# Linear attention and an MLP mixer on one core: attention by quarters of the array, three of nine token-mixing tiles summed onto x in PSUM, and the last block product added onto u

## The chip, the cores and the metric

The kernel runs on one core of a Trainium2 chip. The metric is device time in microseconds. A core has TensorE (PE; its weight loads are listed apart as PEld), VectorE (DVE), ScalarE (ACT), GpSimd (POOL), and SyncE (SP), which here issues nearly all DMAs. [...]

## The reference

```python
kv = einsum('bhsd,bhse->bhde', k, v)          # batch 8, heads 8, seq 576, head_dim 64
out = einsum('bhsd,bhde->bhse', q, kv)
rms = sqrt(mean(out * out, axis=-1) + 1e-6)
x = (out / rms * g_norm) as (8, 576, 512)
h = maximum(x^T @ w_tok1, 0) @ w_tok2          # 576 -> 256 -> 576 along the sequence
u = x + h^T
y = u + maximum(u @ w_ch1, 0) @ w_ch2          # 512 -> 1536 -> 512
```

q, k, v and the results are float32; the four weights come as float64 and are turned into float32 on the chip.

## The kernel before, in words

The work has two parts. The first (up to about 205 us) makes u; the second (up to the end) applies the two channel products by a fast block scheme of two levels, with seven products in the place of eight at each level. The change touches the first part and the last block product of the second.

**First part.** Batches go in pairs: pair 0 to 3, each with two batches ("sides"). The sequence of 576 is four tiles of 128 and a rest of 64; the rests of the two sides share one tile, so a pair has nine tiles of x, 128x512 each. Chunk c of 0 to 3 holds two tiles (sides 0,0,1,1), chunk 4 the shared rest.

For a pair the steps have short names, and the plans `start`, `middle`, `steady(...)` (twice) and `last` are lists of these names, written out by hand. The order of the names is the order in which every engine gets its instructions.

- `kv00` to `kv11` (side, half of the heads): the 64x64 products of k and v, two heads at once, into the two lower or upper column halves of the array (`128*64` in the profile). `l00` to `l11` load the next pair's k and v into the same buffers, `lq0`, `lq1` the next q. `e00` to `e11` copy the result to `kvp`, on DVE for pair 0, on ACT later.
- `a`: attention, q times kv, into an "o" bank. `kvp` holds two heads as a block diagonal of 128x128 with zeros, so that one matmul serves two heads. The zeros come from two memsets of the kv banks at the start.
- `g`: times g_norm, from the bank into x (DVE). `q`: square, from the same bank (ACT). `t`: sum over a head (DVE). `m`, `r`, `i`: mean, root (ACT), inverse (DVE), for a group of chunks. `s` or `p`: x times the inverse, by eight small ACT instructions or one of POOL.
- `h00` to `h11` and `hr` (side, half of the 256): the first token product, into four "h" banks, with the rest's part in `hr` and then a ReLU on ACT. `h010` is one fourth of `h01`.
- `u0` to `u8`: the second token product of one tile into an "h" bank (two matmuls of 128x512; for `u8` four that use half the columns), then x = bank + x on DVE, then a DMA to `u_dram` after each second tile.
- A digit n: n steps of decoding channel weights (ACT once, DVE six times a block). `w..`: the same for token weights. `j14`, `j10`, `j6`, `j2`: so many matmuls of an identity. `c0` to `c4`: transposes of u for the second part. A name with "-" belongs to the pair before.

In `middle` and `steady` the attention of pair n+1 is woven into the token mixing of pair n; `last` has the token mixing of pair 3 alone.

[...] two for "o", two for kv, four for "h". An "h" bank goes round: the fifth tile that asks for one waits until the first has been read.

**Second part.** `outer(place, size, mul, to, ...)` puts one outer block product on a time line of places: seven inner products into banks a, b and c, and between them copies (ACT) and additions (DVE) that leave four results in `to`. For the last group (the rests, g = 8) and the last block product (o = 3) `to` is a buffer r; `last(m, n)` then adds each quarter of r onto xg, and `store_rest` sends tiles of xg out, one half by a DMA of SP and one by a DMA that ACT issues.

Of the kernel before, what the change touches and what calls it, by code (L numbers as in the profile page):

```python
# [19 lines left out]
def kernel(  # L20
# [32 lines left out]
    nc = tc.nc  # L53
# [21 lines left out]
    def pool(name, bufs, side="left", stack=ctx, **kw):  # L75
# [16 lines left out]
          for n, b in (("o", 2), ("kv", 1), ("h", 4))}  # L92
# [10 lines left out]
    kvp = [inp.tile([P, HP, P], F32, name=f"kvp{i}") for i in range(2)]  # L103
# [227 lines left out]
    def attention(pair, groups):  # L331


        acc, bank, stat = {}, {}, {}

        def kv(side, half):
            n = 4 * pair + 2 * side + half
            kk, vv = k_in[n % 4], v_in[n % 4]

            for i in range(2):  # L340
                for j in range(JJ):
                    for h in range(2):
                        r = ds(h * D, D)
                        matmul(kv_ps[half][r, i, r], lhsT=kk[:, j, ds(i * P + h * D, D)],
                               rhs=vv[:, j, ds(i * P + h * D, D)],
                               start=(j == 0), stop=(j == JJ - 1), skip_group_check=True)

        def evict(side, half):
            o = kvp[side][:, 2 * half:2 * half + 2]
            if pair == 0:  # L350
                keep(nc.vector.tensor_copy(o, kv_ps[half]))
            else:
                copy(o, kv_ps[half])

        def attend(c, t):
            side = c // 2
            o = bank[c, t] = ps["o"].tile([P, DM], F32, name="ps_o", tag="o")
            for hp in range(HP):
                matmul(o[:, ts(hp, P)], lhsT=qT[2 * pair + side][:, hp, ts(2 * (c % 2) + t, P)],
                       rhs=kvp[side][:, hp], start=True, stop=True)  # L360

        def attend_rem():
            o = bank[4, 0] = ps["o"].tile([P, DM], F32, name="ps_r", tag="o")
            for hp in range(HP):
                for side in range(2):
                    matmul(o[ds(side * HF, HF), ts(hp, P)],
                           lhsT=qT[2 * pair + side][:, hp, LO:],
                           rhs=kvp[side][:, hp], start=True, stop=True)

        heads = lambda t: t.rearrange("p (h d) -> p h d", d=D)  # L370
        number = lambda c: H if c == 4 else 2 * H
        sq = {}

        def gain(c, t):
            if t == 0:
# [3 lines left out]
            keep(nc.vector.tensor_mul(heads(X[pair, c][:, t]), heads(bank[c, t]),  # L379
                                      g_sb.to_broadcast([P, H, D])))  # L380

        def square(c, t):
            sq[c, t] = work.tile([P, H, D], F32, name="sq", tag="sq", bufs=3)
            keep(nc.scalar.activation(sq[c, t], heads(bank[c, t]), AF.Square))
# [4 lines left out]
        def stats_of(c):  # L389
            g = group(c)  # L390
            at = sum(number(i) for i in g if i < c)
            return [t[:, ds(at, number(c))] for t in stat[g]]

        def total(c, t):
            g = group(c)
            if g not in stat:
                stat[g] = [stats.tile([P, sum(map(number, g)), 1], F32, name=name)
                           for name in ("ms", "root", "inv")]
            keep(nc.vector.tensor_reduce(stats_of(c)[0][:, ts(t, H)], sq[c, t], axis=AX.X,  # L399
                                         op=ALU.add))  # L400
# [20 lines left out]
        def scale(c, t):  # L421
            x, inv = heads(X[pair, c][:, t]), stats_of(c)[2][:, ts(t, H)]
            for i in range(H):
                keep(nc.scalar.activation(x[:, i], x[:, i], AF.Copy, scale=inv[:, i]))  # L424

        def scale_pool(c, t):
            x, inv = heads(X[pair, c][:, t]), stats_of(c)[2][:, ts(t, H)]
            keep(nc.gpsimd.tensor_mul(x, x, inv.to_broadcast([P, H, D])))
# [7 lines left out]
        for c in range(5):  # L436
            for t in range(1 if c == 4 else 2):
                steps |= {f"{n}{c}{t}": do(f, c, t) for n, f in
                          zip("agqtsp", (attend if c < 4 else lambda c, t: attend_rem(), gain,
                                         square, total, scale, scale_pool))}  # L440
# [5 lines left out]
    def token_mixing(pair):  # L446
# [19 lines left out]

        def tok2(i):
            acc_u = ps["h"].tile([P, DM], F32, name="ps_u", tag="h")
            if i < 8:
                for t in range(NTOK):  # L470
                    matmul(acc_u, lhsT=w_tok2[:, t, ts(i % J, P)], rhs=h1[i // J][:, t],
                                     start=(t == 0), stop=(t == NTOK - 1))
            else:
                for t in range(NTOK):
                    for side in range(2):
                        matmul(acc_u[ds(side * HF, HF)], lhsT=w_tok2[:, t, LO:],
                                         rhs=h1[side][:, t],
                                         start=(t == 0), stop=(t == NTOK - 1))
            x = x_of(pair, i)
            tensor_add(x, acc_u, x)  # L480
# [8 lines left out]
        steps |= {f"h01{j}": do(tok1, 0, 1, (j,)) for j in range(J)}  # L489
# [204 lines left out]
    def outer(place, size, mul, to, base=None, act=copy):  # L694
# [31 lines left out]
        def write(i, j, name, n):  # L726
            tensor_add(to(i, j), fit(banks[name]), t[n])
# [13 lines left out]
        at(2, "c", False, True, lambda: act(to(0, 0), fit(banks["c"])))  # L741
        put(place + PLACE[7] + 2, do(write, 1, 1, "b", "u3"))
        at(4, "a", False, True, lambda: read(to(1, 0), 1, 0))
# [448 lines left out]
```

## Time and profile before

| | |
|---|---|
| median of 3 runs | 813.27 us (813.24 to 813.54) |
| profiled execution | 813.68 us, of which span 811.9 us |
| TensorE clock granted | 0.999 |
| PE busy | 796.3 us, 6388 records |
| DVE busy | 690.8 us, 1318 instructions |
| ACT busy | 288.2 us, 805 instructions |
| DMA | 175.43 MB, 216 GB/s over the span |
| one chunk's tile, gain `g` (DVE, 128x512 from PSUM) | 681 ns, 32 times |
| square `q` (ACT, 128x512 from PSUM) | 597 ns, 32 times |
| x = bank + x (DVE, 128x512) | 678 ns, 36 times |
| copy of kvp (ACT, 128x256) | 356 ns, 12 times |
| scaling `s` (ACT, 128x64) | 335 ns, 184 times |

The span runs from the first to the last instruction; the device time has 1.8 us more around it. A line of the profile names the source line, the engine, the operation, what it writes and reads, and its shape. A form such as `128*64 128x64` of a matmul says: 128 rows and 64 columns of the array, and 64 columns of moving data on 128 partitions. `x16` is the number of records; a float32 matmul leaves two. What stands in brackets is the engine's idle time before, and what ended it. Most lines name one of the helpers (`matmul` is L127, `tensor_add` L118, `copy` L124, `dma` L115), so one goes by the names of tiles. TensorE's durations overlap from one record to the next; the distance of the starts is what a matmul costs.

### The profile page before, as it was taken

The numbers are of one execution on the slowest core, as the hardware profiler recorded it, in microseconds if no ns is written. First come the engines' busy times: TensorE is split into PE (matmuls) and PEld (weight loads), VectorE is DVE, ScalarE is ACT, GpSimd is POOL, SyncE is SP. The second block draws the span as 40 slices with busy tenths as digits, with TensorE's granted clock in tenths as the row PEclk, the third lists the DMA queues.
The fourth block names the chain that finished last, engine by engine and source line by source line (L and its number), as shares of the span: only waits on it lengthen the run. The fifth ranks groups of instructions, "written<-read, shape, count | busy, mean of one in ns | idle before, by whom it ended". The sixth has DMA issues, their size and how long they took to land.

```text
span 811.9 us, 16377 instructions
## 1 busy us (share of the span) xinstructions
PE 796.3 (98%) x6388; PEld 704.9 (87%) x6388; DVE 690.8 (85%) x1318; ACT 288.2 (35%) x805; POOL 79.9 (10%) x75
## 2 busy tenths in 40 slices
PE   6999999999999999999999999999999999999997
PEld 6655565543888899999999999999999999999996
DVE  4688989999986978988997997897898899799687
ACT  1355566471120134243234233333424323423331
POOL 1210101010000011003003003001100200300300
PEclk9999999999999999999999999999999999999999
DMA  9999998335458477368558638737836855764642
GB/s 294 324 342 329 341 357 290 131 130 169 166 203 294 169 213 244 131 210 256 174 182 247 211 134 270 238 118 249 268 123 213 249 178 190 239 199 136 202 147 82
DMA packets 97341, 175.43 MB, mean 216 GB/s; under 512 B 7024, under 2 KB 54128, under 8 KB 97264
## 3 DMA queue, kind: packets, MB, share of 16 engines
q1 hardware_dynamic: 95584, 172.65, 65.4%
q10 hardware_dynamic: 1680, 1.74, 0.7%
q8 instruction: 50, 0.82, 0.4%
q14 instruction: 27, 0.22, 0.1%
HBM read 137.79 MB, written 36.57 MB: 215 GB/s over the span
## 4 chain that ended last, share of the span: by engine, by line
PE 88%; DVE 7%; DMA 3%; issue 1%; ACT 0%; SPq 0%; ACTq 0%; DVEq 0%
PE ps_a L127 37%; PE ps_b L127 18%; PE ps_c L127 9%; PE ps_u L127 5%; PE ps_h L127 5%; PE ps_v L127 4%; PE ps_w L127 4%; PE ps_o L127 2%; DMA v_in<-in_v_dram 2%; PE ps_kv L127 2%; DMA k_in<-in_k_dram 1%; DVE w_ch L174 1%; DVE ms L399 1%; DVE w_ch L118 1%; DVE part L187 1%
## 5 line engine op out<-in xcount | busy, mean ns | idle before, releaser
L118 POOL TENSOR_TENSOR v<-v,v 128x384 f32<-128x384 f32 (+1 forms) x48 | 61.4, 1301 | 534.0 <-ACT v L124 494.0
L124 ACT COPY u<-ps_a 128x128 f32<-128x128 f32 (+1 forms) x160 | 56.1, 351 | 156.9 <-PE ps_a L127 156.9
L127 PE MATMUL ps_b<-uT,sums 128*128 128x128 f32 x672 | 86.2, 276 | 0.0
L127 PEld LDWEIGHTS ps_b<-uT,sums 128*128 128x128 f32 x672 | 80.7, 192 | 0.2
L118 DVE TENSOR_TENSOR v<-v,v 128x768 f32<-128x768 f32 (+1 forms) x86 | 79.4, 930 | 1.1
L127 PE MATMUL ps_a<-uT,w_ch 128*128 128x128 f32 x576 | 78.9, 275 | 0.0
L124 ACT COPY ps_c<-ps_a 128x128 f32<-128x128 f32 (+1 forms) x80 | 26.9, 336 | 130.1 <-PE ps_a L127 130.1
L118 DVE TENSOR_TENSOR v<-ps_b,u 128x384 f32<-128x384 f32 x112 | 61.4, 548 | 12.8 <-PE ps_b L127 11.0
L127 PEld LDWEIGHTS ps_a<-uT,w_ch 128*128 128x128 f32 x576 | 71.5, 192 | 0.4
L127 PE MATMUL ps_u<-h,w_tok 128*128 128x512 f32 (+1 forms) x160 | 66.9, 602 | 0.5 <-DVE x L118 0.5
L127 PE MATMUL ps_h<-x,w_tok 128*128 128x512 f32 (+1 forms) x160 | 65.8, 603 | 0.0
L118 DVE TENSOR_TENSOR uT<-uT 128x512 f32<-128x512 f32 (+4 forms) x103 | 63.0, 628 | 0.8
L127 PE MATMUL ps_a<-uT,w 128*128 128x128 f32 x432 | 60.0, 275 | 0.0
L127 PEld LDWEIGHTS ps_a<-uT,w 128*128 128x128 f32 x432 | 54.0, 192 | 0.0
L127 PEld LDWEIGHTS ps_h<-x,w_tok 128*128 128x128 f32 (+1 forms) x160 | 25.9, 189 | 31.1 <-issue 28.3
L118 DVE TENSOR_TENSOR xg<-xg,r 128x512 f32<-128x512 f32 (+1 forms) x78 | 50.8, 663 | 2.3 <-ACT r L124 1.6
L127 PEld LDWEIGHTS ps_u<-h,w_tok 128*128 128x128 f32 (+1 forms) x160 | 24.7, 179 | 30.2 <-issue 22.6
L121 ACT ACTIVATE v<-v 128x384 f32<-128x384 f32 (+1 forms) x86 | 42.6, 528 | 22.8 <-DVE v L118 22.4
L118 DVE TENSOR_TENSOR sv<-v 128x384 f32<-128x384 f32 x80 | 43.3, 549 | 8.4 <-ACT v L121 8.4
L424 ACT ACTIVATE x<-x,inv 128x64 f32<-128x64 f32 x184 | 46.0, 335 | 9.5 <-DVE inv L419 8.1
L127 PE MATMUL ps_a<-sums,sv 128*128 128x128 f32 x336 | 47.0, 276 | 0.0
L127 PE MATMUL ps_a<-uT,sums 128*128 128x128 f32 x336 | 46.8, 276 | 0.0
(128 smaller groups left out, 1589.2 us busy)
## 6 DMA issues: line engine op xcount, KB each, us to landing
sums<-sums SPq DMA_DIRECT2D x112, 576.0 KB, 4.2
qT<-in_q_dram SPq DMA_DIRECT2D x8, 1152.0 KB, 10.1
xt<-u_dram SPq DMA_DIRECT2D x36, 256.0 KB, 3.5
blocks<-y SPq DMA_DIRECT2D x72, 128.0 KB, 2.6
uT<-blocks SPq DMA_DIRECT2D x36, 256.0 KB, 5.2
xg<-u_dram SPq DMA_DIRECT2D x18, 512.0 KB, 4.9
k_in<-in_k_dram SPq DMA_DIRECT2D x16, 512.0 KB, 9.4
u_dram<-x SPq DMA_DIRECT2D x16, 512.0 KB, 3.9
```

The lines of the kernel that those rows point to most:

```text
L118: keep(engine.tensor_tensor(out=o, in0=a, in1=b, op=op))
L121: keep(nc.scalar.activation(o, a, AF.Relu))
L124: keep(nc.scalar.copy(o, a))
L127: keep(nc.tensor.matmul(*a, **kw))
L174: keep(nc.vector.scalar_tensor_tensor(out=bits, in0=raw()[..., 1], scalar=0x80000000, in1=bits, op0=ALU.bitwise_and, op1=ALU.bitwise_or))
L187: keep(nc.vector.scalar_tensor_tensor(out=part[0], in0=raw()[..., 0], scalar=2.0 ** -52, in1=part[0], op0=ALU.mult, op1=ALU.mult))
L399: keep(nc.vector.tensor_reduce(stats_of(c)[0][:, ts(t, H)], sq[c, t], axis=AX.X, op=ALU.add))
L424: keep(nc.scalar.activation(x[:, i], x[:, i], AF.Copy, scale=inv[:, i]))
```

## The change

Attention: `kvp` has no zeros any more (128x64 for two heads, one above the other). A chunk is computed with 64x64 matmuls, in which row half h of the array serves head h of two and column half n serves 64 of the 128 positions of a tile. The two row halves write to different "o" banks, so a chunk's banks are split by the parity of the head and no longer by tile; gain, square and total go by this parity. Kv gets its banks from a ring of two, without memsets.

Token mixing: for tiles 2, 4 and 6 of the first three pairs, and tiles 2 to 8 of the last, a new step `z` copies x into the "h" bank on ACT (`seed`), the matmuls of `u` add onto it, and ACT copies the sum back into x. The other tiles are as before.

Plans: in `start` the first half of h is split and moved ahead of and behind the fourth kv, `j6` and `j2` go, and of the two tiles of a chunk one is scaled by POOL and one by ACT. In all plans one `a` stands for both tiles of a chunk.

End: the last block product of all puts its four results onto xg with additions straight from PSUM.

```diff
-          for n, b in (("o", 2), ("kv", 1), ("h", 4))}
+          for n, b in (("o", 2), ("kv", 2), ("h", 4))}
...
-    kvp = [inp.tile([P, HP, P], F32, name=f"kvp{i}") for i in range(2)]
+    kvp = [inp.tile([P, HP, D], F32, name=f"kvp{i}") for i in range(2)]
...
+            o = kv_ps[side, half] = ps["kv"].tile([P, 2, D], F32, name="ps_kv")
...
-                        matmul(kv_ps[half][r, i, r], lhsT=kk[:, j, ds(i * P + h * D, D)],
-                               rhs=vv[:, j, ds(i * P + h * D, D)],
+                        at = ds(i * P + h * D, D)
+                        matmul(o[ds(h * D, D), i], lhsT=kk[:, j, at], rhs=vv[:, j, at],
                                start=(j == 0), stop=(j == JJ - 1), skip_group_check=True)
...
-        def attend(c, t):
+        def attend(c):
+            o = [ps["o"].tile([P, 2, HP, D], F32, name="ps_o", tag="o") for _ in range(2)]
             side = c // 2
-            o = bank[c, t] = ps["o"].tile([P, DM], F32, name="ps_o", tag="o")
-            for hp in range(HP):
-                matmul(o[:, ts(hp, P)], lhsT=qT[2 * pair + side][:, hp, ts(2 * (c % 2) + t, P)],
-                       rhs=kvp[side][:, hp], start=True, stop=True)
+            for t in range(2):
+                for hp in range(HP):
+                    for n in range(2):
+                        for h in range(2):
+                            r = ds(h * D, D)
+                            matmul(o[h][ds(n * HF, HF), t, hp],
+                                   lhsT=qT[2 * pair + side][r, hp, ds((2 * (c % 2) + t) * P + n * HF, HF)],
+                                   rhs=kvp[side][r, hp], start=True, stop=True)
+            for h in range(2):
+                bank[c, h] = o[h].rearrange("p t k d -> p (t k) d")
...
+                    for h in range(2):
+                        r = ds(h * D, D)
+                        matmul(o[h][ds(side * HF, HF), hp], lhsT=qT[2 * pair + side][r, hp, LO:],
+                               rhs=kvp[side][r, hp], start=True, stop=True)
...
+            x = X[pair, c].rearrange("p t (k h d) -> p (t k) h d", h=2, d=D)[:, :, h]
+            keep(nc.vector.tensor_mul(x, bank[c, h], g_sb.to_broadcast([P, number(c), D])))
...
+        def seed(i):
+            acc[i] = ps["h"].tile([P, DM], F32, name="ps_u", tag="h")
+            copy(acc[i], x_of(pair, i))
+
         def tok2(i):
-            acc_u = ps["h"].tile([P, DM], F32, name="ps_u", tag="h")
+            if i not in seeds:
+                acc[i] = ps["h"].tile([P, DM], F32, name="ps_u", tag="h")
+            first = i not in seeds
...
+                           start=(first and t == 0), stop=(t == NTOK - 1), skip_group_check=True)
...
-            tensor_add(x, acc_u, x)
+            if first:
+                tensor_add(x, acc[i], x)
+            else:
+                copy(x, acc[i])
...
         def write(i, j, name, n):
-            tensor_add(to(i, j), fit(banks[name]), t[n])
+            tensor_add(to(i, j), fit(banks[name]), to(i, j) if onto else t[n])
+
+        def put_on(i, j, n):
+            if onto:
+                tensor_add(to(i, j), to(i, j), t[n])
+
+        def take(i, j, name, act):
+            if onto:
+                tensor_add(to(i, j), banks[name], to(i, j))
+            else:
+                act(to(i, j), fit(banks[name]))
...
+            if g == NG - 1 and o == 3:
+                outer(7 * n, P, mul, lambda i, j: xg[g][:, i, ds(DH + j * P, P)], onto=True)
...
-            put(b + 52, do(last, 1, 1), do(last, 1, 0), do(store_rest, xg, 1))
-            put(b + 53, do(last, 0, 0))
-            put(b + 56, do(last, 0, 1), do(store_rest, xg, 0))
+                                 (52, [do(store_rest, xg, 1)]), (56, [do(store_rest, xg, 0)])):
...
-    kv_ps = [ps["kv"].tile([P, 2, P], F32, name=f"ps_kv{i}") for i in range(2)]
-    for t in kv_ps:
-        keep(nc.vector.memset(t, 0.0))
...
-        "a00 g00 q00", "a01 g01 q01 t00", "a10 g10 q10 t01 m0 r0", "a11 g11 q11 t10 i0 p00 p01",
-        "kv10 j6 t11 m1 r1 e10 i1 s10 p11", "kv11 j2 e11", "h00", "a20 g20 q20", "a21 g21 q21 t20",
-        "h010 t21 m2 r2", "a30 g30 q30 i2 p20", "a31 g31 q31 t30", "h011 t31 m3 r3 p21", "a40 i3 p30 g40 q40 p31",
-        "h012 h013 t40 m4 r4 w21 i4 s40 lq0 l10 l11"]
+        "a0 q00 g01 q01 g00 t00 t01 m0 r0", "a1 g11 q10 i0 g10 q11 p00 s01 t10 t11 m1 r1",
+        "kv10 e10 i1 p10 s11", "h000 h001", "kv11 e11", "h002 h003",
+        "a2 q20 g21 q21 g20 t20 t21 m2 r2", "h010 h011", "a3 g31 q30 i2 g30 q31 p20 s21 t30 t31 m3 r3",
+        "h012", "a4 i3 p30 s31 q40 g41 q41 g40 t40 t41 m4 r4", "h013 w21 i4 s40 lq0 l10 l11"]
...
-            "h10 1 t00 t01 2", "h11 4", "hr 2", "a10 g10 q10 a11 g11 q11 1", "kv10 l10 e10 t10 t11 m0 r0 1",
-            "u0 i0 1", "kv11 l11 e11", "u1 1 s00", "u2 1", "a20 g20 q20 a21 g21 q21 s01", "u3 t20 t21",
-            "u4 1", "a40 g40 q40 lq0 s10", "u5 t40 1", "a30 g30 q30 a31 g31 q31 lq1 s11",
+            "h10 1 t00 t01 2", "h11 4", "hr 2 z2", "a1 q10 g11 q11 g10 1", "kv10 l10 e10 t10 t11 m0 r0 1",
+            "u0 i0 1", "kv11 l11 e11", "u1 1 s00", "u2 z4 1", "a2 q20 g21 q21 g20 s01", "u3 t20 t21",
+            "u4 1 z6", "a4 q40 g41 q41 g40 lq0 s10", "u5 t40 t41 1", "a3 q30 g31 q31 g30 lq1 s11",
...
-        "h00 c0 2 -s40 2", "h01 c1 2", "h10 c2 2", "h11 c3 2", "hr 1", "u0 1", "u1 1", "u2", "u3 1", "u4 1",
-        "u5 1", "u6 1", "u7 c4", "u8"]
+        "h00 c0 2 -s40 2", "h01 c1 2", "h10 c2 2", "h11 c3 2", "hr 1", "u0 z2 1", "u1 z3 1", "u2 z4",
+        "u3 z5 1", "u4 z6 1", "u5 z7 1", "u6 z8 1", "u7 c4", "u8"]
```

In `middle` the step `z2` stands behind `u0`, `z4` behind the third kv and ahead of `s00`, and `z6` behind `u4`.

## The prediction

> **What bounds the kernel now.** I read the page's first part, then the windows cut at the stages, then TensorE's timeline inside one stage, then who waits for whom. A stage is one pass of the hand-written plan; the cuts are the first kv products of pairs 1, 2 and 3 (39.91, 80.30 and 126.04 us), the first h product of the last plan (172.41) and the first channel product (204.85).
>
> ```profile
> PE 796.3 (98%) x6388; PEld 704.9 (87%) x6388; DVE 690.8 (85%) x1318; ACT 288.2 (35%) x805; POOL 79.9 (10%) x75
> ```
> ```profile
> 17.00:39.91 22.91, 21.37 (x200) 15.71 (x198) 15.01 (x38) 7.66 (x20) 5.13 (x5) 1.00 1.09 319
> 39.91:80.30 40.39, 39.60 (x305) 23.00 (x306) 34.60 (x68) 21.22 (x60) 2.04 (x2) 1.00 1.02 335
> 80.30:126.04 45.74, 45.74 (x322) 26.07 (x320) 41.58 (x71) 28.09 (x87) 2.76 (x2) 1.00 1.07 351
> 126.04:172.41 46.37, 46.08 (x322) 26.00 (x318) 44.84 (x67) 27.68 (x80) 2.76 (x2) 1.00 0.51 185
> 172.41:204.85 32.44, 31.92 (x82) 13.08 (x80) 32.16 (x40) 10.12 (x30) 3.03 (x2) 1.00 0.49 155
> ```
> Columns: stretch, length, busy of PE, PEld, DVE, ACT, POOL, clock, DMA share, GB/s. TensorE is busy throughout, so time taken from it counts, until something else is as full. Three things nearly are: the DMA engines until 126 us (share over 1), and DVE from 126 to 205 us (77.0 of 78.8 us).
>
> ```profile
> 90.08 1.95 PE L127 MATMUL ps_o<-kvp,qT 128*128 128x128 f32 x16
> 91.86 8.95 PE L127 MATMUL ps_h<-x,w_tok 128*128 128x512 f32 x24
> 100.74 2.05 PE L127 MATMUL ps_o<-kvp,qT 128*128 128x128 f32 x16
> 102.72 1.39 PE L127 MATMUL ps_kv<-v_in,k_in 128*64 128x64 f32 x40
> 104.03 1.98 PE L127 MATMUL ps_u<-h,w_tok 128*128 128x512 f32 x4
> ...
> 116.11 1.09 PE L127 MATMUL ps_r<-kvp,qT 128*64 128x128 f32 x16
> 117.14 1.12 PE L127 MATMUL ps_u<-h,w_tok 128*128 128x512 f32 x2
> ```
> From start to next start: an attention chunk (16 records, 8 matmuls) costs 1.78 us, or 1.98 ahead of kv; kv's 40 records cost 1.31; the remainder chunk 1.03. A fp32 matmul leaves two records.
>
> [...] In kv the single records start in pairs 6 to 7 ns apart, one pair each 58 ns: two column tiles at once. The row-tiled remainder of h starts its pairs 7 ns apart too. From kv's last record to the next full matmul is 152 ns, against 58 inside. [...] Kv is one matmul per 58 ns on average, so the trace leaves open whether twice that rate can be issued. [...] ACT's square waits for DVE's product of the same bank, 41.4 us in 24 waits.
>
> **Part 1, attention in quarters.** A chunk becomes 32 matmuls of 64x64 (64 records) over four tiles of the array. If all four run together at kv's step, that is 16 steps x 58 ns = 0.93, plus 0.15 for the switch of mode: 1.08 us, 0.70 less. The remainder becomes 32 records: 8 x 58 ns + 0.15 = 0.62, 0.41 less. A pair saves 4 x 0.70 + 0.41 = 3.2 us of TensorE, four pairs 12.9. Bounds for a chunk: below, 0.93; above, 3.86 if no two ran together. I take 1.08, since both halves of it (two columns, two rows) are seen to overlap.
>
> A chunk now takes both o banks, so the next chunk waits for both gains and squares; in exchange ACT and DVE start on different banks, where they stood in line. Queued behind that wait are all of TensorE's later products. The remainder's gain, square and total become two halves each: 2 x 0.42 for 0.67 on DVE, some 0.3 us a pair more. Kv's evictions halve, the two memsets at 0.9 us go (under the first load's 6 us): nothing.
>
> **Part 2, x put in PSUM.** Sixteen DVE additions of 0.678 us go (three each in the first three pairs, seven in the last): -10.8 us of DVE. ACT gets 32 copies of about 0.59 (its 128x512 copies out of PSUM): +19 us, onto 10 to 28 us of each 32 to 46 us stage. TensorE now waits for ACT, in order, before u2, u4 and u6, and for the copy out before the bank is used again.
>
> **What the plan makes of it, by stage.** *Start:* half of h goes ahead of the fourth kv, and the fillers between go. But the second q lands at 29.75 and pair 1's first v at 37.8 us; both stay. The plan reaches kv00 at about 37.9 instead of 39.91: -2.0. *Pair 1:* 3.2 less, but u4 is soon done while ACT stands in 16 scalings (4 us) ahead of the last kv eviction, and the third and fifth chunk wait for two banks: about 1.3 of stalls, -1.9. *Pair 2:* u3 takes the bank of u2, which ACT frees only after its scalings s00, and those wait for DVE's inverse:
> ```profile
> 154.78 0.34 DVE L414 RECIPROCAL inv<-root 128x32 f32<-128x32 f32 x1
> ...
> 155.61 0.35 DVE L419 RECIPROCAL inv<-root 128x32 f32<-128x32 f32 x1
> ```
> ```profile
> 156.00 2.02 ACT L424 ACTIVATE x<-x,inv 128x64 f32<-128x64 f32 x8 [1.80 <-DVE inv L419]
> 157.93 1.14 ACT L163 ACTIVATE w_ch<-raw 128x1024 f32<-128x1024 f32 x1
> ```
> That is pair 3, where u2 ended near 156.5 and could end 1.4 earlier now: ACT is not there before 158, and u3, due near 156.2, starts near 158.7, 0.4 later than before. The removed additions give most of it back by the next chunks. Pair 2 has the same with less lag on DVE: -2.2 there, and -1.5 in pair 3. *Last plan:* u4 takes u0's bank, whose addition DVE ended at 195.86 (TensorE stood 0.52 there). DVE's work from 126 to there, 69.5 us, shrinks by only 3 x 0.68 less 0.3, that is 1.7, and then ACT must put x in (0.7 with the signal). So u4 starts 1.0 earlier than in step with pair 2's end, and most of pair 3's gain is lost again: both together -1.1. What is late next is u0's addition on DVE.
>
> **Part 3, the tail.** TensorE's last record starts at 805.71; then the old kernel has an ACT copy at 806.76, held by two DMA issues on ACT's own queue (805.26 to 806.72), and the last DMA issues at 808.11. The new one adds straight from PSUM: six additions of 0.28 on DVE, three of them ahead of the last 0.68 one, so the first stores go out at 806.1 instead of 805.26. The last write is done at 806.9, but each queue still issues four DMAs of 0.5 to 0.87 us after 806.1, the last again near 808.1: 0, between -0.4 and +0.4.
>
> **Sum:** -2.0 - 1.9 - 2.2 - 1.1 - 0 = -7.2. The profiled execution took 813.68 us (span 811.9), 0.4 over the median of 813.27; the sum is a difference, so I set it on the median: 806.1. The channel part from 205 to 800 us has TensorE at 100% and is not touched.
>
> **Rivals.**
> *A: only two quarters at a time.* Issue or the weight path holds the rate to kv's, one matmul each 58 ns. A chunk is then 32 x 58 ns + 0.15 = 2.02: +0.24, or +0.04 ahead of kv: 12 x 0.24 + 4 x 0.04 + 0.2 for remainders = +3.2. ACT's copies in u's way add 0.5 each in three pairs, DVE's relief and the tail return about 1.2: 816.8, slower. It decides from 1.63 us for a chunk's 64 records, 26 ns a record. For it: no stretch shows more than one matmul per 58 ns. Against: starts 6 ns apart, and row and column overlap each shown. If no two overlap, +2 us x 16: 844.
> *B: ACT's queue costs more.* Each of u2, u4, u6 behind 2 to 4 us of scalings, and each two-bank wait 0.5 more: pairs 1 to 3 keep 1 us each, the last none: 810.3.
> *C: the loads bind.* Until 126 us DMA's share is over 1 at 320 to 351 GB/s, so landings hardly move. The seventh q landed at 127.3 for a product at 135.8, due at 129.7 in my sum; the third at 46.8 for 51.7, due at 49.7. There is 2 to 3 us left, so C binds only if all else went better, and holds the gain under about 9.5: 803.8. If raw weights and k slip as well, pairs 1 and 2 give nothing: 810.
> *D: the change does nothing to speak of*: gains in pairs eaten by C and B at once: 812.8.
>
> **Numbers.** Main case 806.1 (803.5 to 809), chance 0.55; B and C on the faster side 0.17; D 0.06; A 0.18 and without any overlap 0.04. Range 803.0 to 817.0: it leaves out the no-overlap case and the ends of the main one. A measurement of this kernel tells about 0.2% (1.6 us) from no change. Faster 0.72, same 0.06, slower 0.22.
>
> **What would show it.** Right: a chunk's 64 records within 1.1 us in groups of four, kv00 of pair 1 at 38, of pair 2 near 76.4, of pair 3 near 120, the first channel product near 197.7, TensorE's new idle time before u3 and before chunks three and five ended by ACT, and u4 of the last plan waiting for ACT. Wrong: chunk records 29 ns apart or more (A), PE waiting for qT or v_in (C), a last DMA issue more than 0.5 us off its distance from the last matmul.

## The result and the profile after

The changed kernel takes 813.63 us (median of four executions, 813.18 to 815.80), the kernel before beside it 813.29; the ratio is 1.0009, 95% interval 0.9991 to 1.0027. A second set of twelve executions (below) gives 1.0005, 0.9997 to 1.0013. So there is no change that a measurement of this kernel can tell, where 7.2 us less were forecast. The profiled execution took 815.80 us, span 813.9. It is the longest of its four, and e11 below shows what sets it apart.

From the page of the changed kernel, the busy times, the row of the granted clock, and one of the DMA queues:

```profile
PE 786.6 (97%) x7204; PEld 689.5 (85%) x7204; DVE 681.5 (84%) x1308; ACT 308.1 (38%) x863; POOL 77.0 (9%) x72
...
PEclk9999999999999999999999999999999999999998
...
q8 instruction: 57, 0.93, 0.5%
```

TensorE is busy for 9.7 us less, where the sum had 12.9 (6.8 us at half the clock, shown below, put some 3.4 back); DVE has 9.3 less to do, about as the sum wanted, and ACT 19.9 more. None of it is in the span. TensorE has 816 records more, and a queue that carries instructions (q8) has 57 packets where it had 50. The windows, cut at the same marks as before (pair 1, pair 2, pair 3, last plan, first channel product):

```profile
17.00:42.72 25.72, 19.44 (x398) 12.17 (x396) 14.49 (x38) 11.54 (x36) 3.18 (x3) 0.93 1.09 297
42.72:84.63 41.91, 38.62 (x514) 20.06 (x515) 33.44 (x69) 26.58 (x80) 1.06 (x1) 0.96 1.00 320
84.63:127.88 43.25, 42.99 (x530) 22.40 (x528) 39.85 (x70) 29.25 (x90) 2.79 (x2) 1.00 1.07 363
127.88:173.50 45.62, 43.68 (x530) 22.36 (x526) 43.65 (x67) 29.78 (x87) 2.79 (x2) 1.00 0.54 198
173.50:206.52 33.02, 31.92 (x83) 13.08 (x81) 31.95 (x38) 17.12 (x43) 3.05 (x2) 1.00 0.49 154
```

The clock is the third number from the right. It is below 1.00 in the first two windows, where it never was before. By stage, in us, with a second profiled execution of the changed kernel (e11, 813.25 us) beside the first:

| stage | before | after | after, e11 | forecast | measured | e11 |
|---|---|---|---|---|---|---|
| start, to the first kv of pair 1 | 39.91 | 42.72 | 42.69 | -2.0 | +2.8 | +2.8 |
| pair 1 | 40.42 | 41.91 | 39.34 | -1.9 | +1.5 | -1.1 |
| pair 2 | 45.71 | 43.25 | 43.24 | -2.2 | -2.5 | -2.5 |
| pair 3 and last plan | 78.81 | 78.64 | 78.64 | -1.1 | -0.2 | -0.2 |
| the rest, to the end of the span | 607.04 | 607.41 | 607.55 | 0 | +0.4 | +0.5 |

The rest is the same channel work in every run here but for the tail. It takes between 606.88 (e9) and 608.28 us (e7), so +0.4 there is no more than the spread.

TensorE's timeline in pair 2, where the forecast of the stage came near:

```profile
94.47 1.16 PE L127 MATMUL ps_o<-kvp,qT 64*64 64x64 f32 x64
95.56 9.05 PE L127 MATMUL ps_h<-x,w_tok 128*128 128x512 f32 x24
...
118.53 0.69 PE L127 MATMUL ps_r<-kvp,qT 64*64 64x64 f32 x32
119.16 1.98 PE L127 MATMUL ps_u<-h,w_tok 128*128 128x512 f32 x4
```

A chunk costs 1.09 us from start to start (1.08 forecast), the remainder 0.63 (0.62). The single records come in fours, 6 to 8 ns apart, one four each 58 ns: all four quarters of the array run at once.

The fourth chunk of the start and what follows it, in the kernel before, where TensorE waits no more than 0.18 us:

```profile
33.98 1.95 PE L127 MATMUL ps_o<-kvp,qT 128*128 128x128 f32 x16
35.77 1.02 PE L127 MATMUL ps_h<-x,w_tok 128*128 128x512 f32 x2
36.97 1.09 PE L127 MATMUL ps_r<-kvp,qT 128*64 128x128 f32 x16 [0.18 <-ACT sq L384]
```

The same view of the changed kernel, in the start and at u0 of pair 1, where the time went:

```profile
20.96 0.68 PE L127 MATMUL ps_o<-kvp,qT 64*64 64x64 f32 x29 [1.47 <-ACT sq L396]
21.90 0.80 PE L127 MATMUL ps_o<-kvp,qT 64*64 64x64 f32 x35 [0.25 <-issue]
...
34.09 1.16 PE L127 MATMUL ps_o<-kvp,qT 64*64 64x64 f32 x62
38.11 0.30 PE L127 MATMUL ps_o<-kvp,qT 64*64 64x64 f32 x2 [2.86 <-issue]
38.34 2.07 PE L127 MATMUL ps_h<-x,w_tok 128*128 128x512 f32 x2
40.35 1.39 PE L127 MATMUL ps_r<-kvp,qT 64*64 64x64 f32 x32
41.66 1.13 PE L127 MATMUL ps_h<-x,w_tok 128*128 128x512 f32 x2
42.72 1.39 PE L127 MATMUL ps_kv<-v_in,k_in 128*64 128x64 f32 x40
...
55.62 1.12 PE L127 MATMUL ps_u<-h,w_tok 128*128 128x512 f32 x2
58.66 4.51 PE L127 MATMUL ps_u<-h,w_tok 128*128 128x512 f32 x6 [1.92 <-DVE w_tok L118]
```

The fourth chunk stops after record 62 of 64 and stands 2.86 us. The profile names no bank, no load and no engine for it: "issue" is time for which it has no releaser. Behind it the same work takes twice as long: two records of h 2.01 us instead of some 1.0, the remainder 1.31 instead of 0.63. In stretches of a microsecond and less, the clock is 0.50 from 38.2 to 41.6, and again from 58.7 to 62.1, behind a wait of 1.92 us for w_tok2 that was not there before.

Two things in the trace point to instructions. Over the whole run there is one packet of 16,384 bytes on that queue for each 126 records of TensorE (57 for 7204), and one of them begins at 35.35 us, ends at 36.64 and is followed by record 63 at 38.11. And the small stop in the second chunk comes after 221 records counted from the first kv, the large one after 474: 253 apart, two packets' worth. That these packets carry TensorE's instructions, a matmul record and its weight load each, some 252 a packet (a block, below; its end is an edge), is a reading of the counts; the profile says of the queue only that it carries instructions. These two, 0.25 and 2.86 us, are the only stops of TensorE over 0.04 us without a releaser among 57 packets, so nearly all packets pass without a stop that shows; but the larger of the two costs more than the start was to gain.

Three theories for the runs. **S**, the start: TensorE runs out of instructions, and the halved clock behind that and what it delays eat the gain of the first two stages. **R**, its rival: the seeds and the waits for two banks on ACT eat it everywhere. **D**, added later for pairs 2, 3 and the last plan: DVE's queue sets the pace, so that time taken from TensorE there buys nothing.

### The profile page after: what moved, and what is told of

It reads as the page before. It is cut to its first block, busy times and chain, and to the rows that moved or that the text cites. A ratio compares the mean times of both kernels' runs of the same rounds, so it can differ in the third digit from the quotient of the medians.

```text
span 813.9 us, 18057 instructions
## 1 busy us (share of the span) xinstructions
PE 786.6 (97%) x7204; PEld 689.5 (85%) x7204; DVE 681.5 (84%) x1308; ACT 308.1 (38%) x863; POOL 77.0 (9%) x72
## 3 DMA queue, kind: packets, MB, share of 16 engines
q10 hardware_dynamic: 1680, 1.74, 0.7%
## 4 chain that ended last, share of the span: by engine, by line
PE 84%; DVE 8%; DMA 4%; ACT 3%; issue 1%; ACTq 0%; DVEq 0%
PE ps_a L127 37%; PE ps_b L127 18%; PE ps_c L127 9%; PE ps_v L127 4%; PE ps_w L127 4%; PE ps_h L127 4%; PE ps_u L127 4%; ACT x L438 2%; DMA qT<-in_q_dram 1%; DMA v_in<-in_v_dram 1%; PE ps_o L127 1%; DMA k_in<-in_k_dram 1%; DVE ms L412 1%; DVE x L392 1%; PE ps_kv L127 1%
## 5 line engine op out<-in xcount | busy, mean ns | idle before, releaser
L127 PE MATMUL ps_u<-h,w_tok 128*128 128x512 f32 (+1 forms) x160 | 69.7, 620 | 3.8 <-DVE w_tok L118 1.9
L438 ACT ACTIVATE x<-x,inv 128x64 f32<-128x64 f32 x208 | 52.2, 338 | 11.3 <-DVE inv L431 11.3
L118 DVE TENSOR_TENSOR xg<-xg,r 128x512 f32<-128x512 f32 x74 | 49.9, 684 | 0.6
```

The costliest lines, as they stand in the source:

```text
L118: keep(engine.tensor_tensor(out=o, in0=a, in1=b, op=op))
L127: keep(nc.tensor.matmul(*a, **kw))
L438: keep(nc.scalar.activation(x[:, k, h], x[:, k, h], AF.Copy, scale=inv[:, h, k]))
```

## The experiments

Unless it says otherwise, each is compared with the kernel before, run on the same chip in the same rounds (813.7 to 813.8 us).

### e1: row halves

```diff
-                    for n in range(2):
-                        for h in range(2):
-                            r = ds(h * D, D)
-                            matmul(o[h][ds(n * HF, HF), t, hp],
-                                   lhsT=qT[2 * pair + side][r, hp, ds((2 * (c % 2) + t) * P + n * HF, HF)],
-                                   rhs=kvp[side][r, hp], start=True, stop=True)
+                    for h in range(2):
+                        r = ds(h * D, D)
+                        matmul(o[h][:, t, hp], lhsT=qT[2 * pair + side][r, hp, ts(2 * (c % 2) + t, P)],
+                               rhs=kvp[side][r, hp], start=True, stop=True)
```

> Each attention chunk of the changed kernel in row halves instead of quarters: 16 matmuls of 64 rows by 128 columns instead of 32 of 64x64, same banks, same plan; the remainder chunk stays in quarters. Theory S (TensorE runs out of instructions in the start: in the changed kernel a 16 KB instruction packet begins at 35.35 us, as its 2.86 us stall begins, and the clock is halved after it): with half the records a chunk still takes 1.09 us, the stall in the fourth chunk is gone, granted clock back to 0.999, first kv of pair 1 at 38 to 40 us, whole time 808 to 811. Theory R (ACT's seeds and the waits for two banks eat the gain): nothing changes, 813 to 814. If two row halves do not run at once, a chunk takes 1.9 us and the whole 815 or more.

Measured: 824.67 us, ratio 1.0129 (1.0116 to 1.0143). TensorE's timeline of it:

```profile
21.25 3.05 PE L127 MATMUL ps_o<-kvp,qT 64*128 64x64 f32 x32 [1.45 <-ACT sq L394]
...
33.08 2.00 PE L127 MATMUL ps_o<-kvp,qT 64*128 64x64 f32 x32
35.02 1.98 PE L127 MATMUL ps_h<-x,w_tok 128*128 128x512 f32 x4
```

A chunk costs 1.94 us: the third case of the expectation. The stop in the fourth chunk is gone with half the records, as S said, but the clock is halved behind the 1.45 us wait of the second chunk (22.0 to 28.8 us) and twice more, so the time says nothing on S. It does say that quarters were needed: half the instructions at the same rate was not to be had.

### e2: the old start

`attention_old` is the function of the kernel before; the plan `start` is its too, and `kvp` and the kv banks have its shape.

```diff
-    attentions = [attention(0, ((0,), (1,), (2,), (3,), (4,)))]
+    attentions = [attention_old(0, ((0,), (1,), (2,), (3,), (4,)))]
```

> The first pair's attention and the plan of the start are those of the kernel before (full array, fillers j6 and j2, evictions of whole blocks); pairs 1 to 3, token mixing and tail are the changed kernel's. Theory S: no stall, clock 0.999, first kv of pair 1 at 39.9 to 40.3; pair 1 then takes 38.5 to 40, pair 2 43.3, pair 3 45.6; whole time 808.5 to 811. Theory R: the start matters little, the later pairs keep the loss: 812.5 to 814.

Measured: 810.25 us, ratio 0.9961 (0.9948 to 0.9975). Its windows, cut as above from pair 1 on:

```profile
39.90:78.74 38.84, 36.93 (x514) 19.44 (x515) 33.38 (x67) 24.62 (x72) 2.05 (x2) 1.00 1.01 339
78.74:121.98 43.24, 43.00 (x530) 22.40 (x528) 39.93 (x70) 29.23 (x90) 2.79 (x2) 1.00 1.07 355
121.98:167.58 45.60, 43.68 (x531) 22.37 (x527) 43.68 (x67) 29.72 (x87) 2.79 (x2) 1.00 0.57 206
167.58:200.60 33.02, 31.91 (x82) 13.07 (x80) 31.96 (x38) 17.10 (x43) 3.06 (x2) 1.00 0.49 153
```

S. Start and clock are those of before, pair 1 gives 1.6, and pairs 2, 3 and the last plan are the changed kernel's to 0.02 us. So the start alone, with what it delays in pair 1, holds 3.4 us (813.63 to 810.25), or 3.8 to 4.0 when each kernel is set against the kernel before of its own set. The waits for two banks, the other half of R, are all still there in the later pairs, so R falls as the cause of this loss.

### e3: no seeds

The z steps leave the plans.

```diff
-    mixings = [token_mixing(p, (2, 4, 6) if p < B // 2 - 1 else range(2, 9)) for p in range(B // 2)]
+    mixings = [token_mixing(p, ()) for p in range(B // 2)]
```

> The changed kernel with no x put into PSUM: all nine tiles of u are added by DVE as before; quarters and tail stay. Theory S: start and its stall as in the changed kernel, clock 0.993; pairs 2 and 3 within 1 us of it; the last plan may lose what DVE's seven additions cost; 812.5 to 815. Theory R: the waits for ACT before u3 and u4 go (1.8 us) and ACT comes sooner to the squares: 809.5 to 811.5.

Measured: 813.65 us, ratio 0.9999 (0.9991 to 1.0007): S, and R falls for the seeds. TensorE stands 2.87 us after record 62 of the fourth chunk here too. Pair 3 and the last plan take 78.58 us without seeds, 78.64 with them: the waits for ps_u on ACT go, and waits of 1.31 and 1.62 for squares and 0.56 for DVE's addition of u0 come.

### e4: the tail alone

The kernel before with the changed last block product (`onto`) and its stores.

> The kernel before with the changed tail alone: the last block product of all is added onto u straight from PSUM and its stores go out later. Both theories: within 0.4 us of the kernel before, 812.9 to 813.7. If the tail has lost time by itself: 814 or more, with the last stores later behind the last matmul.

Measured: 814.17 us, ratio 1.0006 (0.9997 to 1.0014): the time is that of the second case, but its interval does not tell it from nothing, and the last store starts 2.11 us behind the start of TensorE's last record, not later than the 2.40 before. From there to the end of the span are 6.33 us here, 6.40 in the changed kernel, 6.18 before.

### e5: four filler matmuls less

```diff
-        "kv00 e00 l00 j14 w01 ...
+        "kv00 e00 l00 j10 w01 ...
```

> The changed kernel with ten filler matmuls instead of fourteen after the first kv: eight records less on TensorE before everything else (the second kv waits for its load there anyhow). Theory S says that TensorE runs out of instructions after a fixed number of them: the stall of 2.9 us with no releaser, after record 62 of the fourth attention chunk, moves by eight records, past the two of h behind it, to the fourth record or so of the remainder chunk, and is about as long less what the extra work takes; the small stall in the second chunk moves from record 29 to about 37. Time 812 to 814.5. If the stall is due to something in that chunk (a bank, a load, the records themselves), it stays at record 62.

Measured: 810.88 us, ratio 0.9965 (0.9951 to 0.9979), under the 812 to 814.5 expected; clock 0.998, nowhere halved until the last matmuls of the run. TensorE's timeline:

```profile
33.74 1.16 PE L127 MATMUL ps_o<-kvp,qT 64*64 64x64 f32 x64
34.83 1.13 PE L127 MATMUL ps_h<-x,w_tok 128*128 128x512 f32 x2
36.43 0.32 PE L127 MATMUL ps_r<-kvp,qT 64*64 64x64 f32 x2 [0.47 <-ACT sq L396]
37.15 1.13 PE L127 MATMUL ps_r<-kvp,qT 64*64 64x64 f32 x30 [0.40 <-DVE x L392]
38.21 1.12 PE L127 MATMUL ps_h<-x,w_tok 128*128 128x512 f32 x2
39.27 1.39 PE L127 MATMUL ps_kv<-v_in,k_in 128*64 128x64 f32 x40
```

The fourth chunk runs through. In the single records the small stop is now after record 37 of the second chunk, eight later and so after 221 in all; it has shrunk to 0.23 us from start to start (0.47 in the changed kernel). After 474 there is 0.35 us from start to start. The packet ends at 36.24 and the next record starts at 37.60, 1.36 behind it, against 1.47 in the changed kernel. So the edge moved as S said, and the restart came hardly sooner (37.60 for 38.11). But in front of the edge there is now a chunk's end, 1 us of h and two waits that TensorE has anyway, and so next to nothing is left to stand for. The expectation had seen the edge move past the h, but not the two waits, and not the clock, which is not halved at all without the long stop. Between the two profiled executions the start is 3.45 us shorter and pair 1 1.74 (its six records of u0 and u1: 2.81 instead of 4.51).

### e6: fillers in quarters

```diff
+            for b in range(2):
+                for a in range(2):
+                    matmul(o[a][ds(b * HF, HF), :P], lhsT=ident[ds(a * HF, HF), ds(b * HF, HF)],
+                           rhs=ident[ds(a * HF, HF)], start=True, stop=True)
-            matmul(o[:, :P], lhsT=ident, rhs=ident, start=True, stop=True)
```

> The kernel before with its four groups of filler matmuls cut into quarters (four 64x64 matmuls, all at once on the array, for one of 128x128): the same time on the array and the same loads, 240 records more on TensorE in the first 28 us, nothing else changed. Theory S: stalls with no releaser turn up in the start, 1 to 3 us in all[...]; first kv of pair 1 at 40.5 to 43; time 814 to 817. If the number of instructions does not matter: 39.9 and 813.3 to 814.

Measured: 816.45 us, ratio 1.0031 (1.0021 to 1.0042). TensorE's timeline at the second group of fillers:

```profile
15.22 1.09 PE L127 MATMUL ps_j<-ident 64*64 64x128 f32 x29
17.06 1.74 PE L127 MATMUL ps_j<-ident 64*64 64x128 f32 x51 [0.75 <-issue]
```

40 + 112 + 40 + 29 = 221 records, the same count as in the changed kernel (40 + 28 + 40 + 20 + 64 + 29), on other work at another time. First kv of pair 1 at 41.19, within S; the stop of 0.75 us is a little under the 1 to 3 expected, and the clock was not halved (0.999). More instructions alone made the start 1.28 us longer. The time of all is 0.3% longer; what it has beyond the start lies in the channel part (607.89 us), which the edit does not touch, and within the spread of that part.

### e7: ACT's and DVE's order

From e2, ACT's scalings moved behind squares (`s10`, `s01`, `s00`, `s11` later in their plans), and fewer decoding steps ahead of u0's addition in the last plan.

> The kernel with the old start (first pair as before, quarters and seeds after it), with three orders changed: ACT's scalings of the pair before go behind the squares of the remainder chunk and of the last chunk (pairs 1 to 3), and the last plan puts two to four decoding steps of DVE behind the additions of u0 and u1 instead of ahead. Theory S, second part (pairs 1 to 3 and the last plan lose to ACT's order and to DVE's queue: waits of 1.33, 0.26, 0.74, 1.12 and 1.11 us): these go, 805.5 to 808. Theory D (DVE, 99% busy from pair 3 on, sets the time of that stretch whatever the order): pair 1 gains 1.3, nothing more: 808.5 to 810.

Measured: 811.23 us, ratio 0.9969 (0.9957 to 0.9980); e2, in another set, had 0.9961. TensorE's timeline:

```profile
159.64 0.72 PE L127 MATMUL ps_r<-kvp,qT 64*64 64x64 f32 x32 [2.14 <-ACT sq L396]
160.29 3.60 PE L127 MATMUL ps_u<-h,w_tok 128*128 128x512 f32 x4
...
186.26 16.03 PE L127 MATMUL ps_u<-h,w_tok 128*128 128x512 f32 x40
```

The wait in the last plan is gone (40 records of u in one run), and pair 3 has a longer one instead, with the clock halved behind it. The 1.33 us before the last chunk of pair 1 stayed, and the time lies in neither range, so neither theory had that right. The waits moved and did not go.

### e8: the seeds alone

The kernel before with `seed` and the changed `tok2` and the z steps in the plans, attention and tail as before.

> The kernel before with only the seeds: x put into PSUM by ACT for the same tiles of u as in the changed kernel, attention and tail as before. Theory D (what DVE is spared comes back as waits for ACT): 812.7 to 814, pair 3 and the last plan together 78 to 79 us. If DVE's relief is worth what it frees (10.8 us of additions, of which seven lie on the path at the end): 810 to 812.

Measured: 811.96 us, ratio 0.9979 (0.9971 to 0.9987): the second case, not the one given to D. Its windows for pair 3 and the last plan:

```profile
126.24:172.06 45.82, 45.82 (x323) 25.93 (x319) 43.21 (x65) 30.46 (x86) 2.76 (x2) 1.00 0.51 183
172.06:203.84 31.78, 31.78 (x83) 13.04 (x81) 31.33 (x39) 17.26 (x43) 3.02 (x2) 1.00 0.51 159
```

TensorE has no idle time at all in 77.60 us, and DVE is busy for 74.54 of them. The stretch is 1.22 us shorter than before, so time taken from DVE counts there, as D has it. With quarters added TensorE needs 75.6, DVE 75.6, and the stretch takes 78.6.

### e9: quarters in two pairs only

From e2, pair 3 gets `attention_old` and its plan too, with the z steps of e8, and the tail is that of the kernel before.

```diff
-    attentions += [attention(p, ((0, 1), (2, 3, 4))) for p in range(1, B // 2)]
+    attentions += [(attention if p < 3 else attention_old)(p, ((0, 1), (2, 3, 4))) for p in range(1, B // 2)]
```

> A version built from the runs so far: quarters in pairs 1 and 2 only, the first and the last pair in full-array attention with their old plans, the seeds as in the changed kernel, the old tail. Theory D (in pair 3 and the last plan quarters buy nothing, since DVE and ACT set that stretch; with full attention and seeds it took 77.6 us, with TensorE busy throughout, with quarters and seeds 78.6): first kv of pair 1 at 39.9, pair 1 38.8, pair 2 43.2, pair 3 and last 77.6, whole time 808 to 809.5, about 1 us under the kernel with quarters in pairs 1 to 3. If quarters do buy something in pair 3 once the start is right: slower than that kernel, 810.5 to 812.

Measured: 808.39 us, ratio 0.9935 (0.9923 to 0.9948). First kv of pair 1 at 39.94, pair 1 38.95, pair 2 43.25, pair 3 and last plan 77.59. D, and the shortest full kernel of these.

### e10: less for DVE

```diff
-            steps += block[2:]
+            steps += [lambda: None] * 6 if blocks is channel and n in (9, 11) else block[2:]
```

> The kernel with the old start and quarters in pairs 1 to 3, with DVE's share of the decoding of two blocks of w_ch left out (twelve instructions, 11.5 us of DVE, at the plan places of pair 3 and the last plan; ACT's scaling stays, so the weights of these blocks are not the reference's). Theory D: the waits of TensorE in that stretch (0.74 before u3, 1.12 before the last chunk, 1.11 before u4 of the last plan) are DVE's queue, two of them seen through ACT: 78.6 us becomes 75.8 to 76.8, whole time 807 to 808.5. If ACT's own order makes the waits, they stay: 78 to 78.7, 810.

Measured: 807.86 us, ratio 0.9933 (0.9917 to 0.9948). Windows of pair 3 and the last plan:

```profile
122.42:166.77 44.35, 43.23 (x530) 22.39 (x526) 37.20 (x60) 29.51 (x87) 2.79 (x2) 1.00 0.60 218
166.77:198.42 31.65, 31.65 (x82) 13.15 (x81) 26.35 (x34) 17.06 (x43) 2.08 (x2) 1.00 0.51 160
```

76.00 us for 78.62: D. The waits before u3 and before u4 of the last plan are gone with DVE's load, although the profile named ACT for both. The third, 1.12 before the last chunk of pair 3, is there unchanged; that one is not DVE's amount of work, and whether it is ACT's order or the two banks was not tried apart.

### e11: the changed kernel again

> The changed kernel once more, unaltered, since its profiled execution of 815.8 us lay 2.2 us over its median. Theory S: TensorE again stands 2.9 us after record 62 of the fourth chunk, and the clock is halved behind it; what an execution of 813.6 us has less is the second halved stretch, after the wait for w_tok in pair 1 (1.7 us), or part of the first: first kv of pair 1 at 41.5 to 43, pair 1 in 40.2 instead of 41.9. If that stall is no fixed part of the kernel: first kv of pair 1 near 39.5.

Measured: 814.20 us, ratio 1.0005 (0.9997 to 1.0013); the profiled execution 813.25. TensorE's timeline:

```profile
33.15 1.16 PE L127 MATMUL ps_o<-kvp,qT 64*64 64x64 f32 x62
37.16 0.27 PE L127 MATMUL ps_o<-kvp,qT 64*64 64x64 f32 x2 [2.86 <-issue]
...
42.69 2.40 PE L127 MATMUL ps_kv<-v_in,k_in 128*64 128x64 f32 x40
```

The same stop at the same record, 2.86 us. Here the clock is halved in one stretch, 38.8 to 45.6; first kv of pair 1 at 42.69, pair 1 in 39.34. The slower clock brings TensorE to u0 1.3 us later and DVE is 1 us earlier, so that w_tok2 is decoded in time: the wait of 1.92 us and the half clock behind it are not there (3.85 us less from the chunk ahead of u0 to the next), the half clock ahead of it costs 1.29 more, and that is the 2.6 us by which the first profiled execution was longer in pair 1.

### e12: quarters alone

> Quarters in pairs 1 to 3 alone: start of the kernel before, no seeds, old tail. Theory D: pair 1 38.9, pair 2 43.1, pair 3 and the last plan together 78.4 to 78.8 as in the changed kernel, with waits for ACT's squares and for DVE's addition in place of those for the seeds; whole time 809.5 to 811, so that the seeds add nothing beside quarters though alone they took 1.8 us off. If seeds and quarters add up: 811.5 to 812.5.

Measured: 809.44 us, ratio 0.9951 (0.9937 to 0.9964). Pair 1 39.24, pair 2 42.99, pair 3 and last plan 78.60: D for that stretch. So quarters in pairs 1 to 3 alone are worth 0.5%, seeds alone 0.2%, and both together with the tail (e2) 0.4%: beside quarters the seeds add nothing.

## Why the prediction was wrong

**Rate of the quarters: right; the saving of TensorE a little too large.** 1.09 and 0.63 us where 1.08 and 0.62 were taken; rival A fell. Nor is kv's 58 ns a matmul a floor for quarters: single records start 6 to 8 ns apart, and a chunk's 32 matmuls come 29 ns each. But a pair saves 2.7 us of TensorE (pair 2: busy 42.99 for 45.71) and not 3.2. The full-array work around a chunk takes longer too: the last record of h or u ahead of the quarters takes 523 ns to the next start, where others take 429, and the first one behind them 533, where it took 432 behind a full-array chunk. The 0.15 us that the prediction took for the switch is only the part inside the chunk; the 523 and 533 stand beside kv in the kernel before too.

**Start, -2.0: the step that failed, with the wrong sign.** The step said that only the second q and pair 1's v bound it. Three things came that it did not price. (1) Instructions: a chunk is 64 records in 1.1 us instead of 16 in 1.8, and the working counted matmuls by their time on the array alone. Its question on issue was whether one instruction can follow another fast enough, not whether instructions arrive. The stop is 2.86 us (e3, e11 the same; gone in e2, next to nothing in e5). (2) The clock: a fall of the clock was put at nothing, without a reason. Behind the stop come 6.8 us at half the clock, in one stretch (e11) or with a second one in pair 1, which is 3.4 us of TensorE's work, though waits take in a part of it. Whether the fillers that went ("the fillers between go") have a part in this is not shown: no run puts j6 and j2 back, the clock is full where they stood, and e5 with four more gone is faster. (3) Even in e5 the start ends at 39.27, 0.64 and not 2.0 sooner than before: the second chunk stands 1.47 us for both banks' squares and the first h 1.34 for POOL's scaling.

**Pair 1, -1.9: right in the main, undone by the start.** With the old start it gives 1.6 (e2: 38.84). Of the stalls that were named, the one before the last chunk came (1.33 us, 0.76 before the change); a wait of 0.56 for w_tok2 came that was not named. In the first execution of the changed kernel it loses 1.92 us at w_tok2's second block and 1.7 by the clock. The wait is there in e5 too, with a start in time; DVE's timeline of e5:

```profile
42.15 0.42 DVE L392 TENSOR_TENSOR x<-ps_r,g_sb 128x256 f32<-128x256 f32 x1 [2.08 <-ACT sq L396]
```

DVE, with the decoding of the last token weights (the rest of w_tok1, then w_tok2) queued behind this product, waits for the remainder's square, and that stands on ACT behind eight scalings (39.83 to 41.85) that POOL did before. In e2 DVE waits there 0.72. The prediction's term for this was the remainder's gain, square and total in two halves, "some 0.3 us a pair more"; in the start it is 1.3 us (that decoding begins 5.26 us behind the first kv of pair 1, in e2 3.93), by the place in the queues and not by the length.

**Pair 2, -2.2: near (-2.5), in part by luck.** The sum was 3.2 saved less 1.0 of stalls; it is 2.7 saved less 0.26, the wait before the last chunk. Two misses stand against each other.

**Pair 3 and last plan, -1.1: mechanism right, size wrong** (-0.2). The waits named are there, in TensorE's timeline of the changed kernel:

```profile
160.88 1.98 PE L127 MATMUL ps_u<-h,w_tok 128*128 128x512 f32 x4 [0.74 <-ACT ps_u L124]
...
166.91 1.16 PE L127 MATMUL ps_o<-kvp,qT 64*64 64x64 f32 x64 [1.12 <-ACT sq L396]
...
197.58 9.00 PE L127 MATMUL ps_u<-h,w_tok 128*128 128x512 f32 x24 [1.10 <-ACT ps_u L124]
```

u3, the last chunk, and u4 of the last plan. u4 was to start 1.0 sooner from the first kv of pair 3 on: it starts 69.70 us behind it, before 69.88. The mis-sized term is DVE's shrinking, 1.7 forecast. Summed over this stretch up to u0's addition in e2, DVE's instructions come to 1.37 less, it stands 0.46 and 0.42 for ACT's square and root, and u0's addition ends 68.96 behind that kv instead of 69.82, 0.86 sooner. ACT's seed takes the rest. (DVE was not quite full there either: up to the end of u0's addition it was busy for 68.03 us of 69.83 before, not for 69.5.) What "B" priced at 1 us a pair was true of this stretch, but by DVE's load and not by ACT's queue (e3, e10).

**Tail, 0 between -0.4 and +0.4: right**, +0.2 from the last matmul on. The first stores go out at 807.45, 0.09 before the last record, and the last at 809.65, 2.11 behind it where it was 2.40; but the last lands 5.43 behind instead of 5.23, perhaps because eight stores now leave within 2.2 us and not 2.9; no run tries that apart.

**Rival D**, "gains in pairs eaten by C and B at once: 812.8", had the number and not the cause: C's loads were not it. The cases of a faster kernel had 0.72 of the chances; the main one and C counted on the gain in the start, and B, which did not, left 1 us in each pair.

## What to carry to other kernels

A matmul cut in four leaves four times the records (64 for a chunk where it had 16), so where cut matmuls stand close together, count records against the packets: here, where TensorE stood at the end of a block of some 126 records, it went on 5.8 (e6) to 7.0 us behind the block's first record (changed kernel: record 348 at 31.1, restart at 38.1). A short stop of TensorE can cost as much again by the clock behind it as by itself (2.86 us, then 3.4 us of work), so price a stop with the clock. And where a second engine is as full as the first in a stage, faster work on the first turns into waits (pair 3 and the last plan: 75.6 us of work on each, 78.6 for the stretch): take the change out of that stage, as e9 does, and keep it where only the first is full.

## What the runs showed of the hardware that I had not expected

**Instructions arrive in blocks, and a block can be late.** In the changed kernel's start, a packet begins 3.8 to 5.1 us after the first record of the block ahead of it, at a DMA share of 1.1, and takes 1.1 to 1.3; TensorE, where it stands for it, goes on 1.5 us behind its end. In e3, e5, e6 and e11 that last step is 1.4 to 1.5 too, so the restart follows the packet from run to run. Whether the loads make the packets late was not tried apart. TensorE stood at the end of a block for a packet that had begun only after it had entered that block (record 348 at 31.1, packet at 35.35), so by this reading no more than the rest of one block lay ahead of it there.

**The clock was halved behind a stop of 1.92 us.** In the changed kernel the trace's stretches of one clock, the first of them from 10.91 us, begin 27.31, 3.41, 17.07 and 3.41 us apart, which is 8, 1, 5 and 1 times 3.41, and the last, at 809.63 us, 747.52 behind the one before, 219 times 3.413; in e1, e3, e7 and e11 the changes lie on such a grid too. TensorE's idle time in single stretches of that grid, and the clock in the next one:

| run | stretch, us | idle in it, us | clock in the next |
|---|---|---|---|
| changed kernel | 34.81 to 38.22 | 2.86 | 0.50 |
| e3 | 35.19 to 38.60 | 2.48 | 0.50 |
| e7 | 156.76 to 160.17 | 2.14 | 0.50 |
| changed kernel | 55.29 to 58.70 | 1.92 | 0.50 |
| e12 | 158.37 to 161.79 | 1.62 | 1.00 |
| changed kernel | 17.74 to 21.15 | 1.47 | 1.00 |
| e5 | 50.65 to 54.06 and 54.06 to 57.48 | 0.77 and 1.13 | 1.00 and 1.00 |

So the stop of 1.92 us lay whole in one stretch and cost the clock, and the stop of 1.90 us in e5 was cut in two by the grid and did not. In this table 1.92 us of a stretch of 3.41 had the half clock behind it, and 1.62 had not. The row halves of e1 stay out of this: there the clock fell behind stretches with 1.45, 1.58 and 1.71 us, and no run shows why.

**The step of a matmul went with the wider of what it loads and what it moves, not with the number of tiles.** Where both are 64 wide, one step is 58 ns: in kv (two 128x64 tiles at once) and in quarters (four 64x64). Where one of them is 128, it is 110 to 112 ns: in the row halves of e1 (two 64x128 tiles, 7 ns apart, 64 moved), in the remainder chunk of the kernel before (two 128x64 tiles, 128 moved) and in full attention (128 and 128). The two tiles of 64x128 gave a chunk of 1.94 us, no gain on the full array's 1.78. This is a reading that fits these five numbers; no run was made to separate the two widths.
